# Attention through packed keys, then a squared-ReLU layer: another order for everything up to batch 1's first layer

## The chip, the cores and the metric

The kernel runs on one core of one Trainium2 chip. The metric is the device time of one execution in microseconds (us). A profile is one execution recorded by the hardware profiler. Its span is counted from the first to the last recorded instruction; the time of the execution is a little longer.

The core's engines are TensorE (PE in the profile; PEld is its weight loads), VectorE (DVE), ScalarE (ACT), GpSimd (POOL) and SyncE (SP). Each works through its own list of instructions in order and waits on semaphores of the others.

## What is computed

Eight batches of eight heads, 576 queries, keys and values of width 64, and 32 pack vectors `p` for each head. All inputs are float32.

```python
def sm_attn(qq, kk, vv):
    s = scale * np.matmul(qq, kk.transpose(0, 1, 3, 2))
    s = s - np.max(s, axis=-1, keepdims=True)
    a = np.exp(s)
    a = a / (np.sum(a, axis=-1, keepdims=True) + 1e-09)
    return np.matmul(a, vv)
p_packed = sm_attn(p, k, v)
out = sm_attn(q, p_packed, p_packed)
```

The result, brought to 4608 rows of 512, is `x`; the output is `relu(x @ w_in)**2 @ w_out` with `w_in` 512 x 2048 and `w_out` 2048 x 512.

## The kernel before, in words

The heads of a batch are handled as two quads of four. The first attention gives a packed matrix of 32 rows for each head; since it is key and value of the second one, `x @ w_in` is worked out as `a2 @ (packed @ w_in)`: the products "wp" of the packed matrix with W_in come first, and layer 1 multiplies the second softmax with them. The 576 tokens of batches 0 and 1 are cut into a first part of 256 and a second part of 320 (`CUTS`), and their softmax is done in these parts.

**The order is written out by hand.** `ORDER` (line 50) is a string of words, and `run` (line 768) turns each word into instructions in turn. Every engine executes its instructions in the order in which the words name them. A word may end in the engine for its vector work (`:v` VectorE, `:a` ScalarE, `:p` GpSimd); without an ending it is VectorE, or whatever the step has fixed. The first digit behind the letters is the batch, the next one the quad. The words that matter here:

- `Lk`, `Lv`: load keys, values (line 288). `LA`, `LB`: load both quads' queries of a batch, tokens of the first or second part (272). `Wi`n c: load a piece of W_in (253); n is the columns 0 to 255, 256 to 511 or 512 to 1023 of the half c. `Wo`: load a quarter of W_out (260). All of these are issued on the POOL queue, in front of and between GpSimd's own work. `pf`: load `p` of batches 0 and 1 on the SP queue. `Pr`, `Px`, `Pt`, `Pu`: the other batches' `p`.
- `I`: the identity for transpositions by TensorE, made on GpSimd. `P0`, `P1`: scale, cast and transpose `p` of batch 0 or 1 (VectorE, lines 231 and 235).
- `Z`n.m: n idle products of 512 columns and m of 256 on TensorE (line 331). Nothing reads them.
- First attention: `kT` transposes keys (VectorE, 351), `s1` scores (TensorE, 375), `m1` maximum (VectorE, 401), `x1` exponential (ScalarE, 413), `eT` transposes it on TensorE (433) and `eo` copies that out (421 on VectorE, 419 on ScalarE), `rd` reciprocal (444), `pv` product with the values (457), `pp` the scaled result (470), `bd` its transposition on VectorE (478), `pt` and `po` the one on TensorE and its copy (496).
- Second attention, A for the first part and B for the second: `qA`, `qB` transpose queries (VectorE, 363), `zA`, `zB` scores of both quads (TensorE, 375), `tA` transposes them (518), `mA` maximum (523), `sA` subtraction (529), `xA` exponential (ScalarE, 535), `uA` sum and reciprocal (541, 543), `aA` scaling (549), `TA` transposition (563), and the same with B.
- `wa`, `wb`, `w0`, `w1`: products with columns 0 to 255, 256 to 511, 0 to 511, 512 to 1023 of both halves of W_in (574); `Wa` and so on copy them out.
- Layer 1: `h`b.part.block is a product of two matmuls (590), `r` its relu (595 on ScalarE, 597 on VectorE), `q` the square of a pair of blocks (633 ScalarE, 635 VectorE or GpSimd). Layer 2: `o`tile.j two matmuls (648), `c` the copy out, `d` the store (679).

The POOL queue's loads use eight semaphores in turn, so that a load waits until the one eight places before it has landed. PSUM is shared out twice: before the first `h` three banks for attention and one for idle products, from the first `h` on two banks "x" and two "y" (`STAGES`). A product of batch 0's layer 1 takes a bank of x or y by the parity of its block and waits until the relu that last read that bank is through. Two larger buffers hold scores and wp products in turn.

Of the kernel before, what the change touches and what calls it, by code (L numbers as in the profile page):

```python
# [59 lines left out]
r0.1.15:v h0.1.4 r0.0.7:a Lv20 h0.1.6 m110 r0.1.4:a h0.1.5 r0.1.6:a h0.1.7 m111 h0.1.12 q0.0.3:a o2.0 x110 r0.1.5:v o2.1  # L60
r0.1.12:v q0.1.7:p o0.0 x111 o3.0 r0.1.7:a eT10 q0.1.6:a o0.1 Pr q0.1.2:v eT11 q0.1.3:v eo10:a o1.0 rd1 eo11:v o3.1 pv1
o1.1 pp1 o0.2 pt1 o1.2 bd1 po1:a o3.2 qA11 w011 w111 qA10 W011:a o0.3 W111:v o2.2 Lv21 o1.3 qB10 zA1 qB11 w010 o2.3 tA11
W010:a tA10 o3.3 mA11 zB1 mA10 sA11 w110 o0.4 sA10 tB11 W110:a o2.4 tB10 o1.4 mB11 xA11 o0.5 xA10 mB10 o1.5 uA10 o2.5
Lk20 sB11 o0.6 uA11 o0.7 xB11 aA10 o1.6 c0:a aA11 o1.7 sB10 o3.4 TA10 c1:a d0 TA11 o2.6 uB11 xB10 h1.0.1 Lk21 h1.0.6 Px
o2.7 r1.0.1:v d1 r1.0.6:v o3.5 aB11 h1.0.0 c2:a h1.0.2 Pt o3.6 r1.0.0:a TB11 o3.7 r1.0.2:a d2 Lk31 Pu:v q1.0.0:a h1.0.4
h1.0.3 c3:a o4.0 r1.0.3:v r1.0.4:a o5.0 kT20 q1.0.1:a h1.0.7 d3 h1.0.5 uB10 o5.1 r1.0.5:a o4.1 r1.0.7:v q1.0.2:a aB10
# [31 lines left out]
h4.0.10 q4.0.6 r4.1.2:a pv5 d17 r4.0.10:a h4.0.7 Lv61 q4.1.1 h4.0.15 r4.0.7:a o19.0 q4.0.5 r4.0.15:a pp5 o19.1 q4.0.3
o19.2 Lv71 bd5 h4.0.8 pt5 bs5:v h4.1.11 r4.0.8:a o18.3 po5:v q4.0.4 h4.1.1 s25 r4.1.11:a r4.1.1:v o18.4 qT60 h4.1.0
o18.5 t251 h4.1.6 o19.3 r4.1.0:a t250 r4.1.6:a o18.6 q4.1.0 h4.0.14 h4.1.10 m251 r4.0.14:a w050 r4.1.10:a w150 q4.0.7  # L100
W050:a h4.1.4 m250 h4.1.7 o18.7 r4.1.4:v W150:a o19.4 r4.1.7:v o19.5 q4.1.5 c18:a o19.6 q4.1.3 sb50:v o19.7 d18 h4.1.8
qT61 c19:a o20.0 x250 h4.1.5 sb51:v o21.0 d19 r4.1.5:a o20.1 r4.1.8:a su50 o21.1 x251 h4.1.12 q4.1.2 h4.1.9 r4.1.12:a
# [720 lines left out]
```

## Time and profile before

| | us |
|---|---|
| median of 3 runs | 243.33 (243.23 to 243.66) |
| time of the profiled execution | 243.35 |
| its span | 241.5 |
| TensorE busy | 235.4 |
| VectorE busy | 203.0 |
| ScalarE busy | 142.0 |
| GpSimd busy | 74.8 |

A row of the timeline gives start, duration, engine, line, operation, what is written and read, the number of instructions merged, and in brackets the idle time of the engine before it and what ended it. A row of the table by stages gives the stretch and its length, then busy time and number of instructions of PE, PEld, DVE, ACT and POOL, the granted clock, the share of the DMA engines and their GB/s. Line numbers are those of the kernel before; in the changed kernel each is two higher, since `ORDER` has two lines more.

### The profile page before, as it was taken

To read this page: it belongs to the slowest core of one execution; us is meant where nothing else is said; L and a number is where in the kernel's file an instruction comes from. 1 tells how busy PE (TensorE), PEld (TensorE's weight loads), DVE (VectorE), ACT (ScalarE), POOL (GpSimd) and SP (SyncE) were. 2 spreads that over 40 slices of the span, in tenths; PEclk is the share of its full clock that TensorE was granted. 3 is DMA by queue.
4 is the path that set the end of the run, shared out by engine and by line. 5 is a ranking of instruction groups with operands and counts; after the bars stand their busy time and mean duration, and the time that the engine had idled before them with its cause. 6 is when DMAs were issued, how large, how long until landed. Compare 5 with 4: busy or idle time off the path is not lost.

```text
span 241.5 us, 6098 instructions
## 1 busy us (share of the span) xinstructions
PE 235.4 (97%) x2415; PEld 125.9 (52%) x2415; DVE 203.0 (84%) x459; ACT 142.0 (59%) x308; POOL 74.8 (31%) x123
## 2 busy tenths in 40 slices
PE   8998899999999999999999999999999999999994
PEld 3544564456544564456555554465545644555542
DVE  2679986999998889989998889997899879987740
ACT  2216993697897557955693647774495346733300
POOL 8637783594585262044303340002000000000000
PEclk9999999999999999999999999999999999999999
DMA  6999999999999979259932974217113111111224
GB/s 103 189 199 210 202 206 206 181 209 210 194 169 212 236 103 136 51 71 209 107 86 28 206 107 66 62 34 105 37 24 76 46 46 43 43 46 43 50 61 109
DMA packets 33404, 28.51 MB, mean 118 GB/s; under 512 B 8160, under 2 KB 28384, under 8 KB 33376
## 3 DMA queue, kind: packets, MB, share of 16 engines
q0 software_dynamic: 26848, 18.55, 54.2%
q1 hardware_dynamic: 6384, 9.51, 14.8%
q8 instruction: 19, 0.31, 0.5%
q14 instruction: 9, 0.07, 0.1%
q10 hardware_dynamic: 144, 0.07, 0.1%
HBM read 37.22 MB, written 9.44 MB: 193 GB/s over the span
## 4 chain that ended last, share of the span: by engine, by line
PE 91%; DMA 4%; ACT 2%; DVE 1%; SPq 0%; issue 0%; POOL 0%; POOLq 0%
PE ps_o L648 50%; PE ps_h L590 26%; PE ps_wp L574 4%; PE ps_idle L335 3%; PE ps_s L375 3%; DMA k_b<-in_k_dram 2%; PE ps_e1T L433 2%; PE ps_pv L457 1%; DMA out_dram<-o_sb 1%; ACT r L595 1%; ACT wp L419 1%; SPq L679 0%; PE ps_ppT L496 0%; ACT gT L633 0%; DVE kT L351 0%
## 5 line engine op out<-in xcount | busy, mean ns | idle before, releaser
L648 PE MATMUL ps_o<-w_out_bf,gT 128*128 128x512 bf16 (+1 forms) x576 | 147.3, 378 | 0.0
L590 PE MATMUL ps_h<-a2T,wp 128*128 128x288 bf16 (+2 forms) x512 | 89.9, 286 | 1.3 <-DVE rs L543 0.6
L595 ACT ACTIVATE r<-ps_h 128x288 bf16<-128x288 f32 (+2 forms) x159 | 61.0, 415 | 47.2 <-PE ps_h L590 42.5
L648 PEld LDWEIGHTS <-gT 128*128 128x128 bf16 x576 | 54.4, 98 | 43.1 <-issue 3.4
L590 PEld LDWEIGHTS <-wp 128*128 128x128 bf16 x512 | 47.7, 98 | 42.4 <-issue 8.0
L597 DVE TENSOR_SCALAR r<-ps_h 128x288 bf16<-128x288 f32 (+2 forms) x97 | 41.9, 447 | 11.1 <-PE ps_h L590 10.5
L635 DVE TENSOR_TENSOR gT<-r 128x576 bf16<-128x576 bf16 (+2 forms) x104 | 45.1, 446 | 2.8 <-ACT r L595 1.8
L419 ACT CAST wp<-ps_wp 128x1024 bf16<-128x1024 f32 (+1 forms) x29 | 27.7, 974 | 9.0 <-PE ps_wp L574 8.9
L419 ACT COPY o_sb<-ps_o 128x512 f32<-128x512 f32 x26 | 15.2, 589 | 12.3 <-PE ps_o L648 10.1
L268 POOL DMA_DIRECT2D k_b<-in_k_dram x28 | 15.2, 544 | 16.5 <-DVE kT L351 7.3
L268 POOL DMA_DIRECT2D q_b<-in_q_dram x16 | 11.0, 690 | 28.8 <-DVE qT L363 25.4
L313 POOL DMA_DIRECT2D v_b<-in_v_dram x12 | 9.4, 779 | 31.5 <-PE ps_pv L457 30.5
L335 PE MATMUL ps_idle<-gT 128*128 128x512 bf16 (+1 forms) x59 | 16.1, 417 | 1.2 <-DVE gT L187 1.2
L413 ACT ACTIVATE e<-ps_s,nm 128x576 bf16<-128x576 f32 x16 | 11.8, 742 | 7.5 <-DVE nm L401 7.4
L633 ACT ACTIVATE gT<-r 128x512 bf16<-128x512 bf16 (+1 forms) x21 | 14.0, 690 | 0.5 <-DVE r L597 0.3
L535 ACT ACTIVATE e<-d 128x576 f32<-128x576 f32 (+2 forms) x20 | 11.7, 599 | 4.1 <-DVE d L529 3.9
L351 DVE STREAM_TRANSPOSE kT<-k_b 128x576 uint32<-128x576 uint32 x16 | 12.3, 767 | 0.6 <-DMA k_b<-in_k_dram 0.6
L363 DVE STREAM_TRANSPOSE qT<-q_b 128x576 uint32<-128x576 uint32 (+2 forms) x20 | 12.4, 633 | 0.0
L541 DVE TENSOR_REDUCE sums<-e 128x18 f32<-128x576 f32 (+2 forms) x20 | 12.2, 608 | 0.1
L401 DVE TENSOR_REDUCE nm<-ps_s 128x1 f32<-128x576 f32 x16 | 11.5, 739 | 0.8 <-PE ps_s L375 0.7
L523 DVE TENSOR_REDUCE mx<-s 128x18 f32<-128x576 f32 (+2 forms) x20 | 11.6, 609 | 0.0
L529 DVE TENSOR_TENSOR d<-s,mx 128x576 f32<-128x576 f32 (+2 forms) x19 | 11.6, 631 | 0.0
(60 smaller groups left out, 179.3 us busy)
## 6 DMA issues: line engine op xcount, KB each, us to landing
out_dram<-o_sb SPq DMA_DIRECT2D x65, 128.0 KB, 2.9
v_b<-in_v_dram POOLq DMA_DIRECT2D x12, 256.0 KB, 5.5
w_out_bf<-in_moe_w_out_dram POOLq DMA_DIRECT2D x4, 512.0 KB, 12.4
q_b<-in_q_dram POOLq DMA_DIRECT2D x6, 288.0 KB, 5.3
q_b<-in_q_dram POOLq DMA_DIRECT2D x12, 144.0 KB, 5.7
k_b<-in_k_dram POOLq DMA_DIRECT2D x12, 108.0 KB, 4.1
gT<-in_v_dram POOLq DMA_DIRECT2D x4, 288.0 KB, 9.7
w_in_bf<-in_moe_w_in_dram POOLq DMA_DIRECT2D x4, 256.0 KB, 9.8
```

The costliest lines, as they stand in the source:

```text
L268: engine.dma_start(x[n:], s[:P - n])
L335: self.nc.tensor.matmul(ps[:, :m], lhsT=self.nought[:, :P], rhs=self.nought[:, :m], start=True, stop=True)
L351: self.nc.vector.transpose(t["kT"][:].rearrange("p s e -> p (s e)").bitcast(U32), t["k"][:].rearrange("p t d -> p (t d)").bitcast(U32))
L363: self.nc.vector.transpose(out.bitcast(U32), x.bitcast(U32))
L419: engine.copy(out, x)
L541: nc.vector.reduce_sum(out=sums[:, x], in_=t["e2"][:, x], axis=AX.X)
L590: self.nc.tensor.matmul(ps, lhsT=t["wp"][:, fb // n, fb % n * P:(fb % n + 1) * P], rhs=t["a2T"][:, s0:s1], start=(qd == 0), stop=(qd == se ...
L595: engine.activation(r, ps, ACT.Relu)
L597: engine.tensor_scalar_max(r, ps, 0.0)
L633: engine.activation(out, r, ACT.Square)
L635: engine.tensor_tensor(out=out, in0=r, in1=r, op=ALU.mult)
L648: self.nc.tensor.matmul(self.o[tt][:, e], lhsT=self.gT[:, fb, a:a + P], rhs=self.w_out_bf[:, fb, e], start=(i == 0), stop=(i == self.NFB - 1))
```

## The change

Only `ORDER` changes. From `h1.0.1`, batch 1's first product of layer 1, on the words are the same in both (an engine that was left to the default is now written out). Before that point the same words stand in another order, except for the idle products, and 30 words have another engine. The beginning, up to batch 1's first scores `s11`:

```diff
-pf Lk00 Lk01 Lv00 Lv01 I P0 LA0 P1 Wi00 kT00 Wi10 LB0 Z18.0 s100 Wi01 kT01 Wi11 m100 Z2.0 s101 x100 m101 Wi21 x101 Z7.0
-eT00 eo00:v Z1.0 eT01 rd0 eo01:v Wi20 Z2.0 pv0 pp0 qA01 Lk10 Z2.0 pt0 bd0 qA00 po0:a Z2.1 zA0 Lk11 tA00 tA01 mA01 mA00
-sA01:v xA01 sA00:v uA01 xA00 qB00 Wo0 qB01 aA01:p uA00 Z18.1 zB0 wa00 Lv11 tB00 tB01 aA00:p Wa00:a mB00 Z2.1 wa01 mB01
-sB00:p Wa01:a TA01 Z1.1 wb01 TA00 Lv10 wb00 xB00 sB01:v h0.0.8 h0.0.9 Wb01:a Wb00:v h0.0.1 h0.0.0 xB01 uB00 r0.0.8:a
-r0.0.1:a h0.0.2 uB01 r0.0.9:a aB00:p r0.0.0:a h0.0.3 r0.0.2:v q0.0.4:a h0.0.11 Wo2 aB01:v h0.0.10 q0.0.0:a TB00 TB01
-r0.0.3:a r0.0.10:v r0.0.11:a h0.1.0 h0.1.1 q0.0.1:v q0.0.5:a h0.1.9 r0.1.0:v h0.1.8 r0.1.1:a r0.1.9:v LA1 w100 w101
-q0.1.0:v r0.1.8:a h0.1.10 W100:v W101:a h0.1.11 h0.1.3 q0.1.4:p h0.1.2 r0.1.10:a r0.1.3:v r0.1.11:a h0.0.4 kT10 r0.1.2:a
-LB1 h0.0.13 r0.0.4:a h0.0.5 q0.1.1:a h0.1.14 r0.0.13:v q0.1.5:p h0.0.14 r0.0.5:v h0.1.13 r0.1.14:a kT11 h0.0.15
-r0.0.14:a h0.0.6 q0.0.2:a h0.0.12 Wo1 r0.0.15:v s11 r0.1.13:a r0.0.12:v r0.0.6:a Wo3 h0.1.15 q0.0.7:v q0.0.6:a h0.0.7
...
+pf Lk00 kT00 Lk01 P0 Z14.0 s100 kT01 m100 x100 I s101 Z2.1 eT00 LA0 m101 x101 qA01 eo00:a Z0.1 eT01 Lv00 qA00 P1 eo01:v
+Lv01 rd0 LB0 Z0.1 pv0 pp0 bd0 Z1.0 pt0 zA0 tA01 qB01 Wi00 qB00 tA00 Wi01 mA01 Wi11 Wi10 mA00 Z6.1 zB0 tB00 Wi20 po0:a
+sA01:v xA01 sA00:v Wi21 xA00 tB01 mB00 uA00 wa01 Lk11 uA01 mB01 wa00 Wa01:a Lk10 sB00:p Wa00:a aA00:p xB00 Z5.1 wb00
+Wb00:a aA01:p TA00 sB01:v xB01 wb01 TA01 h0.0.8 uB00 uB01 Wo0 aB01:v Wb01:a aB00:p Lv10 h0.0.1 Lv11 TB00 h0.0.9 r0.0.8:a
+h0.0.2 h0.0.10 r0.0.1:a r0.0.9:a h0.0.3 h0.0.11 r0.0.2:a h0.0.0 TB01 r0.0.10:a r0.0.11:a q0.0.4:v r0.0.0:a r0.0.3:a
+h0.1.8 q0.0.5:v r0.1.8:v h0.1.0 h0.1.9 q0.0.0:a h0.1.1 r0.1.9:a h0.1.10 r0.1.0:a w100 q0.0.1:v r0.1.1:v Wo2 W100:v w101
+h0.1.11 r0.1.10:a W101:a r0.1.11:v h0.1.2 q0.1.0:v kT11 h0.1.3 r0.1.3:a q0.1.4:p h0.1.14 r0.1.2:a h0.0.5 h0.0.13
+r0.1.14:a LA1 LB1 h0.0.4 h0.0.14 r0.0.5:a kT10 r0.0.13:a h0.1.13 r0.0.4:a h0.1.15 r0.1.13:v h0.0.12 q0.1.1:a r0.0.14:a
+Wo1 r0.0.12:a s11 h0.0.6 h0.0.7 q0.1.5:v r0.1.15:a h0.1.4 m110 r0.0.6:a h0.0.15 m111 r0.0.7:a q0.1.7:p x110 r0.0.15:v
...
```

On the POOL queue the loads now stand in the order keys, queries' first part, values, queries' second part, the four small pieces of W_in, its two large ones, batch 1's keys; before it was keys, values, queries' first part, two small pieces of W_in, queries' second part, the other two, the large ones, batch 1's keys. On VectorE `kT00` goes ahead of `P0`, `P1` behind the queries' transpositions, `bd0` directly behind `pp0`, and the second part's transpositions `tB` between those steps of the first part. `eo00` and `Wb00` go to ScalarE. The idle products are 33 instead of 59: 14 instead of 18 ahead of `s100`, 19 instead of 41 behind it. Between `s11` and `h1.0.1` the old order has seven products `h` of batch 0, the new one eight.

More of the change, by code (lines that the diff above doesn't have):

```diff
@@ L61 @@
[L61 to L65, printed above, removed]
@@ L67 @@
+o2.7 r1.0.1:v d1 r1.0.6:v o3.5 aB11:v h1.0.0 c2:a h1.0.2 Pt o3.6 r1.0.0:a TB11 o3.7 r1.0.2:a d2 Lk31 Pu q1.0.0:a h1.0.4
+h1.0.3 c3:a o4.0 r1.0.3:v r1.0.4:a o5.0 kT20 q1.0.1:a h1.0.7 d3 h1.0.5 uB10 o5.1 r1.0.5:a o4.1 r1.0.7:v q1.0.2:a aB10:v
 h1.0.10 h1.0.8 q1.0.3:v r1.0.10:a o4.2 kT21 Lq2 h1.0.9 r1.0.8:a o5.2 r1.0.9:a h1.0.12 TB10 s12 q1.0.4:v r1.0.12:a
@@ L98 @@
[L98 to L102, printed above, removed]
@@ new lines @@
+q2.1.6:v q2.1.7:v h3.0.5 h3.0.2 qT41 r3.0.5:a o12.6 h3.0.0 r3.0.2:v Lq6 o11.6 r3.0.0:a o12.7 h3.0.1 h3.1.1 r3.0.1:v
+c12:a o11.7 r3.1.1:v s14 d12 c11:a q3.0.0:v h3.0.4 kT50 h3.0.3 r3.0.4:a o13.0 r3.0.3:a m140 d11 h3.0.9 Lk60 o14.0
+r3.0.9:a q3.0.1:v h3.1.3 x140 kT51 h3.1.0 o14.1 r3.1.3:a m141 o13.1 Lk70 r3.1.0:a h3.0.8 q3.0.2:v eT40 x141 h3.0.7
+r3.0.8:v o13.2 eo40:v r3.0.7:a h3.0.6 q3.1.0:v o14.2 q3.0.4:v r3.0.6:a eT41 rd4 q3.0.3:v h3.0.11 eo41:a h3.1.2 r3.0.11:v
+o14.3 r3.1.2:v o13.3 h3.0.12 h3.0.10 q3.1.1:v pv4 r3.0.10:a r3.0.12:v o14.4 Lv51 pp4 h3.0.13 q3.0.5:v h3.0.14 r3.0.13:a
@@ new lines @@
+aT40 aT41 o16.7 qT50 o15.6 c16:a h4.0.1 h4.0.4 Lq7 r4.0.1:v o15.7 d16 r4.0.4:v o17.0 c15:a h4.0.3 h4.0.2 r4.0.3:v o17.1
+r4.0.2:a d15 s15 q4.0.1:v h4.0.0 kT60 h4.0.9 o17.2 r4.0.0:a m151 o17.3 r4.0.9:a h4.0.6 m150 o17.4 r4.0.6:a h4.1.3
+q4.0.0:v x151 o17.5 kT61 o18.0 x150 o17.6 r4.1.3:v Lk71 h4.0.5 h4.0.13 rd5 r4.0.5:a o18.1 r4.0.13:v eT50 h4.0.11 eo50:v
+h4.0.12 eT51 q4.0.2:v o17.7 r4.0.12:v r4.0.11:a o18.2 eo51:a c17:v h4.1.2 h4.0.10 q4.0.6:v r4.1.2:a pv5 d17 r4.0.10:a
+h4.0.7 Lv61 q4.1.1:v h4.0.15 r4.0.7:a o19.0 q4.0.5:v r4.0.15:a pp5 o19.1 q4.0.3:v o19.2 Lv71 bd5 h4.0.8 pt5 bs5:v
@@ new lines @@
+h4.1.11 r4.0.8:a o18.3 po5:v q4.0.4:v h4.1.1 s25 r4.1.11:a r4.1.1:v o18.4 qT60 h4.1.0 o18.5 t251 h4.1.6 o19.3 r4.1.0:a
+t250 r4.1.6:a o18.6 q4.1.0:v h4.0.14 h4.1.10 m251 r4.0.14:a w050 r4.1.10:a w150 q4.0.7:v W050:a h4.1.4 m250 h4.1.7 o18.7
+r4.1.4:v W150:a o19.4 r4.1.7:v o19.5 q4.1.5:v c18:a o19.6 q4.1.3:v sb50:v o19.7 d18 h4.1.8 qT61 c19:a o20.0 x250 h4.1.5
+sb51:v o21.0 d19 r4.1.5:a o20.1 r4.1.8:a su50 o21.1 x251 h4.1.12 q4.1.2:v h4.1.9 r4.1.12:a w151 a250:v r4.1.9:a w051
+h4.1.15 W151:a su51 o20.2 o21.2 r4.1.15:a q4.1.4:v o21.3 W051:a a251:v o20.3 h4.1.14 aT50 h4.1.13 aT51 s16 r4.1.14:a
@@ new lines @@
+q6.0.4:v q6.1.0:v h6.0.12 h6.1.6 r6.0.12:v o28.2 o28.3 r6.1.6:v h6.0.13 o27.4 h6.1.7 r6.0.13:v s27 r6.1.7:a o27.5
+q6.0.6:v t270 h6.1.3 o27.6 r6.1.3:a t271 h6.1.11 o27.7 m270 h6.1.2 r6.1.11:a o28.4 c27:a q6.1.3:v o28.5 r6.1.2:a m271
+h6.1.12 d27 h6.1.4 r6.1.12:a o29.0 q6.1.1:v sb70:v r6.1.4:a o28.6 o29.1 sb71:v x270 o28.7 q6.1.2:v h6.1.8 c28:a su70
+w171 w071 x271 d28 h6.1.9 o30.0 r6.1.8:v W171:a su71 o30.1 o30.2 W071:a a270:v o30.3 h6.1.15 r6.1.9:a a271:v o29.2
+h6.1.10 r6.1.15:a q6.1.4:v o29.3 r6.1.10:a aT70 h6.1.13 h6.1.14 aT71 o30.4 r6.1.13:a q6.1.5:v r6.1.14:a o29.4 q6.1.6:v
@@ L132 @@
+r7.1.8:v o31.7 o32.5 r7.1.3:v c31:a h7.1.10 q7.1.1:v h7.1.6 d31 r7.1.10:v o33.0 r7.1.6:a o32.6 h7.1.12 h7.1.14 o33.1
+r7.1.12:v r7.1.14:a o32.7 h7.1.7 c32:v h7.1.9 r7.1.7:a o33.2 r7.1.9:a h7.1.11 d32 q7.1.3:v o34.0 q7.1.4:v h7.1.13
+r7.1.11:v o33.3 r7.1.13:a o34.1 q7.1.5:v q7.1.6:v h7.1.15 o33.4 r7.1.15:v o33.5 o33.6 q7.1.7:v o34.2 o34.3 o33.7 o34.4
+c33:v o34.5 o34.6 o34.7 d33 o35.0 c34:v o35.1 o35.2 d34 o35.3 o35.4 o35.5 o35.6 o35.7 c35 d35
 """
```

96 lines of the change are left out of this document (41 added, 55 removed).

## Prediction

> **What bounds the kernel now.** First the page: its head, then the busy share of the DMA engines in 40 slices of 6.04 us.
>
> ```profile
> span 241.5 us, 6098 instructions
> ...
> DMA  6999999999999979259932974217113111111224
> ```
>
> The loads keep the DMA engines full from the second slice to the thirteenth, some 78 us. An order of loads can therefore bring one piece earlier only by bringing another later. Next the busy time by stage, at the stage where the two orders meet again (from batch 1's scores `s11` to its first products of layer 1, `h1.0.1`):
>
> ```profile
> 30.00:48.80 18.80, 18.80 (x250) 9.18 (x248) 15.61 (x41) 12.20 (x26) 11.30 (x18) 1.00 1.37 197
> ```
>
> TensorE's column reads 18.80 of 18.80 us. From 30 us on TensorE is the bound, and what it does there is the same in both kernels. So the change can win or lose only ahead of that: by when TensorE reaches batch 1's scores (`s11`), and how much work it still has then. Hence the timeline of TensorE from the first product of layer 1 to `s11`:
>
> ```profile
> 21.28 1.03 PE L590 MATMUL ps_h<-a2T,wp 128*128 128x256 bf16 x8
> 22.90 1.20 PE L590 MATMUL ps_h<-a2T,wp 128*128 128x256 bf16 x8 [0.58 <-DVE rs L543]
> 24.45 1.56 PE L590 MATMUL ps_h<-a2T,wp 128*128 128x320 bf16 x8 [0.35 <-DVE a2T L563]
> 25.93 0.62 PE L574 MATMUL ps_wp<-w_in_bf,ppT 64*32 64x512 bf16 x16
> 26.49 1.26 PE L590 MATMUL ps_h<-a2T,wp 128*128 128x320 bf16 x8
> 28.04 2.54 PE L590 MATMUL ps_h<-a2T,wp 128*128 128x256 bf16 x18 [0.29 <-ACT r L595]
> 30.51 0.70 PE L375 MATMUL ps_s<-kT,pT 32*32 32x192 bf16 x48
> ```
>
> Three waits stand in brackets; ahead of 21.28 TensorE does little but idle products. What releases the first product and the 24.45 row is VectorE, so its timeline comes last:
>
> ```profile
> 7.76 0.78 DVE L351 STREAM_TRANSPOSE kT<-k_b 128x576 uint32<-128x576 uint32 x1 [0.60 <-DMA k_b<-in_k_dram]
> 8.46 1.62 DVE L401 TENSOR_REDUCE nm<-ps_s 128x1 f32<-128x576 f32 x2
> 11.27 0.55 DVE L421 COPY e1T<-ps_e1T 96x768 bf16<-96x768 bf16 x1 [1.19 <-PE ps_e1T L433]
> 11.75 0.15 DVE L444 RECIPROCAL rden<-den 128x2 f32<-128x2 f32 x1
> 11.82 0.55 DVE L421 COPY e1T<-ps_e1T 96x768 bf16<-96x768 bf16 x1
> 12.87 0.42 DVE L470 TENSOR_TENSOR pp<-ps_pv,rden 128x256 bf16<-128x256 f32 x1 [0.49 <-PE ps_pv L457]
> 13.21 0.43 DVE L363 STREAM_TRANSPOSE qT<-q_b 128x256 uint32<-128x256 uint32 x1
> 13.57 0.20 DVE L478 STREAM_TRANSPOSE ppd<-pp 128x64 uint32<-128x64 uint32 x1
> 13.69 0.40 DVE L363 STREAM_TRANSPOSE qT<-q_b 128x256 uint32<-128x256 uint32 x1
> 14.63 0.78 DVE L518 STREAM_TRANSPOSE s<-ps_s 128x256 f32<-128x256 f32 x2 [0.54 <-PE ps_s L375]
> 15.45 0.75 DVE L523 TENSOR_REDUCE mx<-s 128x8 f32<-128x256 f32 x2
> 16.11 0.75 DVE L529 TENSOR_TENSOR d<-s,mx 128x256 f32<-128x256 f32 x2
> 17.01 0.42 DVE L541 TENSOR_REDUCE sums<-e 128x8 f32<-128x256 f32 x1
> 17.46 0.20 DVE L543 RECIPROCAL rs<-sums 128x8 f32<-128x8 f32 x1
> 17.58 0.85 DVE L363 STREAM_TRANSPOSE qT<-q_b 128x320 uint32<-128x320 uint32 x2
> 18.36 0.38 DVE L541 TENSOR_REDUCE sums<-e 128x8 f32<-128x256 f32 x1
> 18.77 0.20 DVE L543 RECIPROCAL rs<-sums 128x8 f32<-128x8 f32 x1
> 19.14 0.91 DVE L518 STREAM_TRANSPOSE s<-ps_s 128x320 f32<-128x320 f32 x2 [0.17 <-PE ps_s L375]
> 19.98 0.84 DVE L523 TENSOR_REDUCE mx<-s 128x10 f32<-128x320 f32 x2
> 20.73 0.49 DVE L563 STREAM_TRANSPOSE a2T<-a 128x128 uint32<-128x128 uint32 x2
> ```
>
> Read it as one chain: the last load of keys (7.76), a stretch of short waits on TensorE, and from 14.63 to 21.22 VectorE with hardly a gap, after which the first product starts at 21.28.
>
> **The change part by part.** All times are in the profiled execution, 243.35 us with its span of 241.5, level with the median of 243.33.
>
> *Keys and first scores: 0.* `Lk00` and `Lk01` are still the first two loads, so the second transposition of keys still waits for its load until 7.76. `kT00` now stands ahead of `P0` on VectorE, which delays `s100`; but the maxima start behind `kT01` at 8.46 in either order.
>
> *`qA01`, `qA00` and `P1` into a gap: 0.* VectorE is idle for 1.19 us ahead of 11.27. The two transpositions of queries take 0.36 + 0.40 there. `P1` is a scaling of 128x128 and a transposition of 128x64, each between nothing and its nearest larger row (0.42 for 128x256, 0.20 for 128x64). All three together end by about 11.4, ahead of `eo01`, since `eo00` goes to ScalarE. Its price there is that of the same copy for batch 1, in the fence below (0.80 against 0.55); ScalarE has nothing else then. If the cover failed, `pv0` would be late by at most the 0.25 between the two.
>
> ```profile
> 22.47 1.20 ACT L595 ACTIVATE r<-ps_h 128x256 bf16<-128x256 f32 x4
> ...
> 35.72 0.80 ACT L419 COPY e1T<-ps_e1T 96x768 bf16<-96x768 bf16 x1
> ```
>
> *Loads: -0.1.* The POOL queue holds eight loads in flight, and its ninth and later ones show when an earlier one is in: the row that waits for the queries' first piece, and the row that waits for their second.
>
> ```profile
> 12.33 0.56 POOL L268 DMA_DIRECT2D k_b<-in_k_dram  x1 [0.73 <-DMA q_b<-in_q_dram]
> ...
> 17.30 0.78 POOL L261 DMA_DIRECT2D w_out_bf<-in_moe_w_out_dram  x1 [1.92 <-DMA q_b<-in_q_dram]
> ```
>
> The first piece (`LA0`) was fifth in line and was in at 12.3. Now it is third and `Lv01` is fifth with the same bytes ahead of it, so the values are in at about 12.2; `pv0`'s second half needs them and `eo01` (12.37), so they barely hide. `pp0` starts near 12.8 instead of 12.87. `LB0`, eighth before, is now sixth: at the page's rate, some 200 KB per us, its 320 KB need 1.6 us, so it is in at 13.8; if it takes the 2.4 that the row at 17.30 would leave it behind two pieces of W_in of 1.3 each, at 14.5. W_in's small pieces follow, two by 17, four by 19.5, where `wa` and `wb` use them; from there on the bytes in line are the old ones.
>
> *`bd0` straight behind `pp0`: -0.45 more.* Now `zA0` waits for the second query transposition to end (13.69 + 0.40 = 14.09), and VectorE reads its result 0.54 later. After the change `zA0` waits for `pp0` (12.8 + 0.34 = 13.14) and, on TensorE, for `pt0` (two products, some 0.4 with the hand-over, an estimate), while `bd0` (0.20) ends beside it: 13.54, and `tA01` starts at 14.08 instead of 14.63.
>
> *VectorE up to `TA01`: +0.1.* From start to start: `tA` 2 x 0.41, `qB` 2 x 0.39, `mA` 2 x 0.33, `sA` 2 x 0.38, sums and reciprocals 2 x 0.58, `tB` 2 x 0.42, `mB` 2 x 0.38, `TA` 2 x 0.25, and one subtraction of the second part (`sB01`) that now stands ahead of `TA01`, 0.45 (an estimate: 1.25 times `sA`'s). Sum 6.7, against 6.59 from 14.63 to 21.22. `TA01` ends near 20.8, and the first product of layer 1 starts there: **0.45 earlier**. `qB01` meets its load (14.5) just in time.
>
> *Second part of the tokens: -0.75 more.* When `TA01` ends, VectorE has done the second part's transpositions, maxima and subtraction; left are two sums (0.6 each), one `aB` (0.5) and two `TB` (0.28 each), so `TB01` ends at 23.0. ScalarE does eight relus in a row from 21.6 (behind the copies of `wb`), 0.30 each by the row at 22.47; the fifth frees the bank that `h0.1.8` needs, at 23.2. So the second part starts at 23.25 instead of 24.45: **1.2 earlier**.
>
> *To `s11` and beyond: +0.25.* Eight products of the second part, W_in's wide half and a third group follow as before, ScalarE and VectorE sharing relus and squares otherwise but in about the same sum (11 relus go to ScalarE and 7 leave it, four squares leave and three come). I carry the 1.2 to `s11`, at 29.3. Behind it the new order has eight products of batch 0 left and the old one seven: one costs 2.54/9 = 0.28. The rest of the way is TensorE's own, so the end comes **0.95 earlier**: 243.35 - 0.95 = 242.4.
>
> *Idle products: 0.* 59 become 33. Those behind `s100` fill waits; 19 of them stand between `zA0` and `zB0` today, and `zB0`'s own operand is ready only at 18.43 anyway.
>
> **TensorE's clock.** The idle products show two speeds:
>
> ```profile
> 5.01 0.15 PEld L335 LDWEIGHTS <-gT 128*128 128x128 bf16 x1 [0.28 <-issue]
> 5.44 1.44 PEld L335 LDWEIGHTS <-gT 128*128 128x128 bf16 x7 [0.28 <-issue]
> ```
>
> Until 5.44 one comes every 0.43 us, then every 0.21: half speed for the first 4.25 us of work (from 1.19). With 23 idle products fewer behind the first scores, TensorE idles for some 5 us more out of 14, in gaps of up to 1.2 us (an estimate from the times above). No row of this trace shows what such gaps do. The Trainium skill, "TensorE: Matmul & The Clock Gate", section "What's actually happening", says that the clock halves only after an idle window of about 3.4 us; by that rule the sum stays 242.4. The same page's section "A second HAM failure mode: psum-queue depth-cycling" speaks against the change: frequent short idling between groups can make the clock swing; by that the third rival below holds.
>
> **The rivals.**
> 1. *The queries' second piece is late.* The change doesn't bring `LB0` in by 14.5. Being sixth speaks for it; that a load behind others took 2.4 us instead of 1.6 speaks against. If it lands at 15.5, `qB01`, which stands second in the VectorE stretch, holds all behind it for 1 us: first product at 21.8, second part at 24.25, `s11` 0.2 earlier at best, and with the one product more the end is where it was: 243.3.
> 2. *Given back to ScalarE.* The relus and squares up to `s11` are on engines that are nearly full from 20 to 32 us. If ScalarE reaches the relus that free the banks 0.6 later than I have it (two relus' worth), the 0.95 falls to 0.35: 243.0.
> 3. *The clock falls* (slower). One mechanism: too little work between 9 and 20 us halves TensorE's clock until 4.25 us of work have passed. Then `zA0` on VectorE's chain takes 0.4 longer and `zB0` delays it by 0.1 (the rest has slack); the first eight products, at 0.43 each, take 3.4 instead of the 2.4 that eight relus take; in the 0.85 left of the 4.25 two products of 320 tokens lose 0.2 each. Together 1.9: 243.35 - 0.95 + 1.9 = 244.3. It outweighs the gain only if the clock is low at the first product of layer 1; low only before that, it costs at most 0.5.
>
> **How the numbers follow.** A measurement of this kernel can tell about 0.2%, 0.5 us. Forecast 0.55: 242.4, between 241.7 (the product left over costs nothing, and the relus don't delay the second part) and 242.85. Rival 1: 0.12. Rival 2: 0.15, half of it beyond 0.2%. Rival 3: 0.13. The remaining 0.05 is a load of W_in or W_out that TensorE now reaches 1 us too early, up to 243.8. Faster by over 0.2%: 0.55 and a part of rival 2, 0.61; within: 0.21; slower: 0.18. The range runs from 241.7 to 244.0: 244.3 and beyond are left out.
>
> **What would show it.** First product of layer 1 at 20.8 and first product of the 320 tokens at 23.25; `tA01` at 14.1 and no load among the releasers of the `qB` transpositions; `s11` at 29.3; TensorE full from there. Wrong are: weight loads of idle products or of the first products 0.43 apart behind 6 us (rival 3), a DMA ahead of `qT` (rival 1), ScalarE as releaser of `ps_h` for more than 0.6 in all between 23 and 30 us (rival 2).

## The result, and the profile after

| | before | after |
|---|---|---|
| median, us | 243.5 (243.23 to 243.71, 4 runs) | 241.76 (241.65 to 242.43, 4 runs) |
| ratio, 95% interval | | 0.9935 [0.9913, 0.9957] |
| profiled execution, its span | 243.35, 241.5 | 241.65, 239.8 |

The changed kernel is faster: by 1.7 us between the medians, by 0.65% (1.6 us) in the ratio. Its page has less busy time on TensorE (fewer idle products) and on VectorE, and more on ScalarE:

```profile
PE 227.4 (95%) x2355; PEld 123.4 (51%) x2389; DVE 200.8 (84%) x455; ACT 144.6 (60%) x313; POOL 73.4 (31%) x122
```

TensorE's timeline, the same places as before:

```profile
12.95 0.36 PE L459 MATMUL ps_pv<-gT,e1T 96*32 96x64 bf16 x24 [0.97 <-DMA gT<-in_v_dram]
...
14.14 0.42 PE L377 MATMUL ps_s<-qT,ppd 32*32 32x256 bf16 x16
...
20.47 0.27 PE L592 MATMUL ps_h<-a2T,wp 128*128 128x256 bf16 x1
21.27 3.96 PE L592 MATMUL ps_h<-a2T,wp 128*128 128x256 bf16 x25 [0.52 <-DVE a2T L565]
...
26.92 2.24 PE L592 MATMUL ps_h<-a2T,wp 128*128 128x320 bf16 x16 [0.22 <-ACT wp L421]
29.09 0.70 PE L377 MATMUL ps_s<-kT,pT 32*32 32x192 bf16 x48
...
47.34 0.60 PE L592 MATMUL ps_h<-a2T,wp 128*128 128x256 bf16 x4
```

The first products of layer 1 start where they did (21.27 against 21.28, one matmul ahead). But then 25 matmuls run in one row, both parts of the tokens in it, where the old order had eight, a wait of 0.58, eight and a wait of 0.35. `s11` comes at 29.09 instead of 30.51, 1.42 earlier, and `h1.0.1` at 47.34 instead of 48.80, 1.46 earlier. A new wait stands at 12.95: the second half of the values. VectorE shows why nothing is won ahead of 21.27 and much behind it:

```profile
13.38 0.42 DVE L472 TENSOR_TENSOR pp<-ps_pv,rden 128x256 bf16<-128x256 f32 x1 [1.23 <-PE ps_pv L459]
13.84 0.25 DVE L480 STREAM_TRANSPOSE ppd<-pp 128x64 uint32<-128x64 uint32 x1
14.63 0.45 DVE L520 STREAM_TRANSPOSE s<-ps_s 128x256 f32<-128x256 f32 x1 [0.55 <-PE ps_s L377]
15.01 0.86 DVE L365 STREAM_TRANSPOSE qT<-q_b 128x320 uint32<-128x320 uint32 x2
...
20.91 0.30 DVE L565 STREAM_TRANSPOSE a2T<-a 128x128 uint32<-128x128 uint32 x1
...
22.97 0.56 DVE L565 STREAM_TRANSPOSE a2T<-a 128x160 uint32<-128x160 uint32 x2
```

`pp0` comes 0.51 later than before (13.38 against 12.87), `tA01` at the same 14.63. From there to the end of `TB01` it is 8.90 us (to 22.97 + 0.56). In the old kernel it was 9.99, from 14.63 to 24.62 (24.06 + 0.56):

```profile
21.52 0.68 DVE L421 CAST wp<-ps_wp 128x512 bf16<-128x512 f32 x1
...
23.36 0.38 DVE L597 TENSOR_SCALAR r<-ps_h 128x256 bf16<-128x256 f32 x1
...
24.06 0.56 DVE L563 STREAM_TRANSPOSE a2T<-a 128x160 uint32<-128x160 uint32 x2
```

The difference, 1.09, is close to the time of two instructions that left VectorE for ScalarE, the copy `Wb00` (0.68) and the relu `r0.0.2` (0.38), 1.06 together. In the changed kernel ScalarE takes eight relus in a row, 0.29 each:

```profile
21.87 2.34 ACT L597 ACTIVATE r<-ps_h 128x256 bf16<-128x256 f32 x8
```

From `s11` to `h1.0.1` both kernels need the same time; the table by stages, the old kernel's row first:

```profile
30.51:48.80 18.29, 18.29 (x246) 8.96 (x245) 15.10 (x40) 11.69 (x25) 10.79 (x18) 1.00 1.37 197
```

```profile
29.09:47.34 18.25, 17.96 (x244) 9.22 (x247) 14.28 (x40) 13.75 (x28) 9.82 (x15) 1.00 1.34 196
```

So the gain is made between `tA01` and `s11` and passes through to the end.

### The profile page after: what moved, and what is told of

Same layout as the page of the kernel before. It is cut to its first block, busy times and chain, and to the rows that moved or that the text cites. A ratio compares the mean times of both kernels' runs of the same rounds, so it can differ in the third digit from the quotient of the medians.

```text
span 239.8 us, 6008 instructions
## 1 busy us (share of the span) xinstructions
PE 227.4 (95%) x2355; PEld 123.4 (51%) x2389; DVE 200.8 (84%) x455; ACT 144.6 (60%) x313; POOL 73.4 (31%) x122
## 4 chain that ended last, share of the span: by engine, by line
PE 85%; DVE 5%; DMA 4%; issue 2%; ACT 2%; POOL 1%; ACTq 0%; POOLq 0%
PE ps_o L650 50%; PE ps_h L592 26%; DMA gT<-in_v_dram 4%; PE ps_wp L576 3%; PE ps_s L377 3%; PE ps_e1T L435 2%; PE ps_pv L459 1%; DVE mx L525 1%; DVE d L531 1%; ACT r L597 1%; DVE s L520 1%; DVE qT L365 1%; PE ps_ppT L498 1%; DVE gT L637 0%; ACT wp L421 0%
## 5 line engine op out<-in xcount | busy, mean ns | idle before, releaser
L650 PE MATMUL ps_o<-w_out_bf,gT 128*128 128x512 bf16 (+1 forms) x544 | 141.3, 378 | 2.0 <-issue 0.5
L597 ACT ACTIVATE r<-ps_h 128x288 bf16<-128x288 f32 (+2 forms) x163 | 61.8, 413 | 48.0 <-PE ps_h L592 43.9
L599 DVE TENSOR_SCALAR r<-ps_h 128x288 bf16<-128x288 f32 (+2 forms) x93 | 40.6, 450 | 11.4 <-PE ps_h L592 10.5
L637 DVE TENSOR_TENSOR gT<-r 128x576 bf16<-128x576 bf16 (+2 forms) x106 | 45.7, 444 | 2.1 <-ACT r L597 1.2
L421 ACT CAST wp<-ps_wp 128x1024 bf16<-128x1024 f32 (+1 forms) x31 | 29.1, 961 | 7.2 <-PE ps_wp L576 7.2
L353 DVE STREAM_TRANSPOSE kT<-k_b 128x576 uint32<-128x576 uint32 x16 | 12.2, 769 | 4.9 <-DMA k_b<-in_k_dram 4.9
L635 ACT ACTIVATE gT<-r 128x640 bf16<-128x640 bf16 (+1 forms) x20 | 13.3, 694 | 0.5 <-DVE r L599 0.3
L576 PE MATMUL ps_wp<-w_in_bf,ppT 64*32 64x512 bf16 (+1 forms) x272 | 10.7, 369 | 1.4 <-DVE s L520 0.8
```

Source lines behind the costliest of these rows:

```text
L421: engine.copy(out, x)
L576: self.nc.tensor.matmul(ps[NP * g:NP * g + NP, c, :f1 - f0], lhsT=t["ppT"][D * c:D * c + D, NP * h:NP * h + NP], rhs=self.w_in_bf[D * c:D ...
L597: engine.activation(r, ps, ACT.Relu)
L599: engine.tensor_scalar_max(r, ps, 0.0)
L635: engine.activation(out, r, ACT.Square)
L637: engine.tensor_tensor(out=out, in0=r, in1=r, op=ALU.mult)
```

## Experiments

Each changes only words of `ORDER`. After the result two theories stood. **Theory E**: the gain comes from the engines, from what left VectorE between `tA01` and `TB01`. **Theory O**: it comes from the order on VectorE, which brings the second part's scores, maxima and the wp products forward. Rival 3, the clock, and the order of the loads were open beside them. One table for all, from the profiled executions: the start of `tA01`, the time from there to `s11`, the time from `s11` to the end of the span, and the median of all runs with the ratio to the kernel before, run beside it.

| kernel | `tA01` | to `s11` | to the end | median | ratio |
|---|---|---|---|---|---|
| before | 14.63 | 15.88 | 210.99 | 243.28 to 243.5 | |
| after | 14.63 | 14.46 | 210.71 | 241.76 | 0.9935 [0.9913, 0.9957] |
| two back on VectorE | 13.54 | 17.39 | 210.77 | 243.38 | 0.9996 [0.9980, 1.0013] |
| new order, old engines | 13.90 | 19.55 | 212.55 | 247.90 | 1.0183 [1.0154, 1.0212] |
| old order, new engines | 14.79 | 17.14 | 211.67 | 245.45 | 1.0097 [1.0074, 1.0120] |
| values first | 15.06 | 15.44 | 210.80 | 241.81 | 0.9943 [0.9918, 0.9968] |
| after, filled | 14.18 | 14.45 | 210.77 | 241.73 | 0.9934 [0.9920, 0.9949] |
| no late idle products | 14.86 | 15.57 | 210.77 | 242.56 | 0.9969 [0.9955, 0.9983] |
| values first, filled | 14.49 | 14.63 | 211.08 | 241.99 | 0.9949 [0.9934, 0.9964] |
| old order, loads only | 14.26 | 15.88 | 210.86 | 243.29 | 1.0001 [0.9991, 1.0011] |
| filled, two back | 14.33 | 15.99 | 210.78 | 242.80 | 0.9972 [0.9960, 0.9983] |
| filled, old VectorE order | 14.20 | 15.82 | 210.78 | 242.54 | 0.9966 [0.9955, 0.9977] |
| values first, `pp0` first | 14.77 | 14.84 | 210.99 | 241.82 | 0.9939 [0.9924, 0.9954] |

Read the columns apart. The last of the three times hardly moves, but for the two kernels where words behind `s11`, too, have an engine chosen for the other order. The first scatters by over a microsecond between kernels with the same words up to `tA01` (13.54 and 14.63), and with it single times. The second shows the mechanism.

**1. Two back on VectorE.**

```diff
-Wb00:a
+Wb00:v
-r0.0.2:a
+r0.0.2:v
```

> The changed kernel with two words back on VectorE: the copy of the second small wp product (Wb00, 0.68 us there) and the relu of h0.0.2 (0.38 us). Theory E (engines: the second part's softmax ends earlier since these two left VectorE): TB01 ends 1.06 us later, the first product of 320 tokens 1 us later, time 241.76 + 1.0 = 242.8. Rival O (order: tB, mB and sB stand earlier, which is what brings the second part forward): at most 0.2 us, 241.8 to 242.0.

Measured 243.38 (242.26 to 243.85): the whole gain is gone, more than these two should cost. The profiled execution (243.48) shows a second thing. On TensorE:

```profile
17.51 0.62 PE L576 MATMUL ps_wp<-w_in_bf,ppT 64*32 64x256 bf16 x15 [1.92 <-DMA w_in_bf<-in_moe_w_in_dram]
18.07 2.53 PE L337 MATMUL ps_idle<-gT 128*128 128x512 bf16 x6
```

and on VectorE:

```profile
21.01 0.69 DVE L423 CAST wp<-ps_wp 128x512 bf16<-128x512 f32 x1 [1.99 <-PE ps_wp L576]
```

A piece of W_in was late, TensorE idled for 1.92, and the six idle products behind it took 2.53, at half the clock; at the full clock these six (five of 512 columns, one of 256) take 1.36. `Wb00`, now on VectorE, waited 1.99 for its product behind them. The mean granted clock was 0.986 to 0.993 in eight of the twelve runs (medians 243.68 in these, 242.54 in the other four). So this run mixes the two instructions with the clock, and experiment 9 repeats it without that.

**2. New order, old engines.** All 30 words get their old engine back; three of them:

```diff
-Wb00:a r0.0.10:a q0.0.4:v
...
+Wb00:v r0.0.10:v q0.0.4:a
...
```

> The words in the new order, all 30 words that changed engine back on their old one. Theory E: the gain of 1.7 us falls to 0.7 or less, 242.8 or more, with VectorE as the releaser of the first product of 320 tokens. Rival O: most of the gain stays, 242.2 or less.

Measured 247.90 (246.89 to 249.26), 4.6 slower than before; 247.0 and 246.89 in the two runs at the full clock. TensorE's waits, summed over the run (who waited for whom: us in all, times, the longest), with the old kernel's line numbers:

```profile
PE ps_h L590 <- DVE r L597: 2.2, 3, 1.6
PE ps_h L590 <- DVE a2T L563: 1.4, 3, 0.9
...
PE ps_h L590 <- DVE wp L421: 1.1, 1, 1.1
```

Each of these names VectorE: it now has relus and copies among the second part's softmax, and TensorE waits for all three kinds of its work. Between them in the list stand 1.4 us for pieces of W_in. At the full clock the order alone costs 3.7. The result is on theory E's side (242.8 or more) and far from theory O's, but a loss as large as this was in neither.

**3. Old order, new engines.** The same 30 words in the old kernel, the other way round (`Wb00:a`, `r0.0.10:a` and so on in the old order).

> The words in the old order with the old idle products, the 30 words on their new engines. Theory E: 242.4 to 243.0 (1.06 us off VectorE, but ScalarE then does Wb00 ahead of xB01, 0.58 us, and 0.25 more for eo00 ahead of pv0). Rival O: no gain, 243.3 or more.

Measured 245.45 (245.39 to 246.90), 2.2 slower. Now it is ScalarE:

```profile
PE ps_h L592 <- ACT r L597: 1.9, 3, 1.1
```

In the old order the copies of the wp products come late on ScalarE, and the relus put behind them start at 23.12 and hold the banks. This is theory O's side (243.3 or more) and 2.5 us beyond theory E's. So experiments 2 and 3 speak for one theory each. Neither half of the change gains alone: order +4.6, engines +2.2, both together -1.7.

**4. Values first.** The first queries are loaded fifth, as in the old kernel, the values third and fourth.

```diff
-... s101 Z2.1 eT00 LA0 m101 x101 qA01 eo00:a Z0.1 eT01 Lv00 qA00 P1 eo01:v Lv01 rd0 LB0 Z0.1 pv0 pp0 bd0 Z1.0 ...
+... s101 Z2.1 eT00 m101 x101 eo00:a Z0.1 eT01 Lv00 P1 eo01:v Lv01 rd0 LA0 qA01 LB0 Z0.1 pv0 pp0 bd0 qA00 Z1.0 ...
```

> The changed kernel with batch 0's values loaded ahead of the queries' first part, as before the change, and the two transpositions of those queries later on VectorE (one behind rd0, one behind bd0). If the wait of 0.97 us for the values at pv0 is on the path: pp0 0.5 us earlier, tA01 at 14.2 to 14.4 instead of 14.63, time 241.3 to 241.5. If it is hidden (the queue only changes which of the two loads is late, or ScalarE's relus set the pace from 21.9 us on): 241.7 to 241.8, with tA01 near 14.6 or the relus where they were.

Measured 241.81 (241.14 to 243.05), no different from the changed kernel. Its seven runs fall apart by the clock: 242.48, 242.89 and 243.05 at a mean of 0.993, and 241.14 to 241.81 at 0.998 and above, medians 1.6 apart. The profiled one is the slowest, and its timeline shows what half a clock does there:

```profile
14.37 0.63 PE L377 MATMUL ps_s<-qT,ppd 32*32 32x256 bf16 x16 [0.31 <-DVE qT L365]
...
17.60 0.48 PE L377 MATMUL ps_s<-qT,ppd 32*32 32x320 bf16 x16
```

`zA0` takes 0.63 instead of 0.42. `zB0` stands behind seven idle products (six of 512 columns, one of 256) and starts 3.23 us after `zA0`, in the changed kernel 1.86 (14.14 to 16.00): at half speed the filling itself is in the way. The clock is not all that is late in this execution: VectorE waits 1.13 us for the queries' first part, until 12.95, and `tA01` is at 15.06.

**5. After, filled.** Eleven more idle products, 44 in all: four ahead of `s100`, one ahead of `pt0`, three ahead of each `wa`.

```diff
-Z14.0 s100 ... Z1.0 pt0 ... uA00 wa01 Lk11 uA01 mB01 wa00
+Z18.0 s100 ... Z2.0 pt0 ... uA00 Z3.0 wa01 Lk11 uA01 mB01 Z3.0 wa00
```

> The changed kernel with 11 more idle products in its gaps: four behind the first fourteen, three ahead of each of wa01 and wa00, one ahead of pt0. Theory C (in some executions TensorE's granted clock falls for one stretch of about 3.4 us, since too few idle products are left; mean clock 0.993 instead of 1.000): mean clock 0.998 or more in every run, times between 241.3 and 242.0, median 241.6. Rival L (the spread of the changed kernel comes from loads that land at other times): the same spread as before the fill, up to 242.5, with mean clocks of 0.993 among the runs.

Measured 241.73 (241.17 to 242.10), level with the changed kernel; the mean clock is 1.000 in each of the six runs (the changed kernel: 1.000, 0.997, 0.993 and 0.993 with 241.65, 241.66, 241.86 and 242.43). The profiled one, 241.17, is the changed kernel's timeline 0.46 earlier, from the values on:

```profile
12.50 0.36 PE L459 MATMUL ps_pv<-gT,e1T 96*32 96x64 bf16 x24 [1.09 <-DMA gT<-in_v_dram]
...
20.81 3.96 PE L592 MATMUL ps_h<-a2T,wp 128*128 128x256 bf16 x25 [0.53 <-DVE a2T L565]
...
28.63 0.70 PE L377 MATMUL ps_s<-kT,pT 32*32 32x192 bf16 x48
```

The values landed 0.45 earlier, and every row behind them and the end (0.48) came that much earlier. Filling holds the clock, but does not move the median here, and at the full clock the six runs still spread over 0.93.

**6. No late idle products.** Only the first 14 are kept; the other 19 go.

```diff
-s101 Z2.1 eT00 ... Z0.1 eT01 ... Z0.1 pv0 ... Z1.0 pt0 ... Z6.1 zB0 ... Z5.1 wb00
+s101 eT00 ... eT01 ... pv0 ... pt0 ... zB0 ... wb00
```

> The changed kernel with only the first fourteen idle products; the other nineteen are left out. Theory C: the clock falls in every execution, mean 0.985 to 0.993, 1 to 2 us slower than 241.7: 242.7 to 243.7. Rival N (idle products only fill waits and do nothing): 241.7 and a mean clock of 1.000.

Measured 242.56 (241.71 to 243.07), 0.8 above the filled kernel. The mean clock is 0.970 to 0.979 in all eleven runs; at 0.979 they take 241.71 to 242.28, at 0.970 to 0.972 they take 242.56 to 243.07. In the profiled one (242.98) the table by stages has the granted clock third from the end:

```profile
8.16:11.57 3.41, 1.82 (x44) 1.29 (x47) 2.92 (x8) 2.34 (x5) 1.10 (x2) 1.00 1.29 201
11.57:25.22 13.65, 8.51 (x132) 4.43 (x133) 10.50 (x32) 6.60 (x17) 7.74 (x12) 0.50 1.30 204
25.22:28.63 3.41, 3.19 (x33) 1.53 (x32) 3.05 (x7) 3.36 (x9) 2.05 (x3) 1.00 1.20 203
```

```profile
16.15 0.73 PE L377 MATMUL ps_s<-qT,ppd 32*32 32x320 bf16 x16 [1.36 <-DVE qT L365]
...
21.49 5.08 PE L592 MATMUL ps_h<-a2T,wp 128*128 128x256 bf16 x25 [0.42 <-DVE a2T L565]
```

The clock falls at 11.57 and is back at 25.22. The block of 25 matmuls, nearly all of it at half the clock, takes 5.08 instead of 3.96. This is rival 3 as it was described, low clock at the first product, at a price of 0.8 in the medians: 1.3 in the six runs at 0.970 to 0.972, 0.3 in the five at 0.979. The clock fell for longer than forecast and cost less.

**7. Values first, filled.** Experiments 4 and 5 together.

```diff
-eT00 LA0 ... Lv01 rd0 LB0 ... uA00 wa01
+eT00 ... Lv01 rd0 LA0 qA01 LB0 ... uA00 Z3.0 wa01
```

> The order with the values ahead of the queries' first part (as in the run of that order), and the same 11 more idle products. Theory C: the runs of that order at full clock (241.14 to 241.32) become all of them, 241.2 to 241.5, and it beats the changed kernel by 0.3 to 0.5. Rival L: still spread from 241.1 to 243, median 241.8.

Measured 241.99 (241.59 to 242.52) at a clock of 0.999 or more: the expected gain is missing. The values are there in time, and now the queries are not:

```profile
12.59 0.45 DVE L365 STREAM_TRANSPOSE qT<-q_b 128x256 uint32<-128x256 uint32 x1 [1.15 <-DMA q_b<-in_q_dram]
```

12.59 against the 12.50 of the values in experiment 5: in these two executions the fifth load in line is waited for, whichever it is. Why the four runs of experiment 4 at the full clock (241.14 to 241.81) were mostly faster than these six is open.

**8. Old order, loads only.** The kernel before with `LB0` ahead of W_in's pieces.

```diff
-LA0 P1 Wi00 kT00 Wi10 LB0 Z18.0
+LA0 P1 LB0 Wi00 kT00 Wi10 Z18.0
```

> The kernel before with one edit: the queries' second part loaded ahead of all pieces of W_in. By the reading that the new load order is worth nothing without the order on VectorE (there qB00 starts only behind uA01, at 17.58, and its load was in at 17.3): 243.2 to 243.6. By the reading that the load itself is the gain: 242.5 or less.

Measured 243.29 (242.75 to 243.69), ratio 1.0001 [0.9991, 1.0011]. The earlier load alone is worth nothing. It was in by 14.24, when the load that takes over its semaphore starts, against 17.30 before; but in the old order nothing asks for it before 17 us.

**9. Filled, two back.** Experiment 1 on the filled kernel.

```diff
-Wb00:a ... r0.0.2:a
+Wb00:v ... r0.0.2:v
```

> The changed kernel with the 11 more idle products, and Wb00 and the relu of h0.0.2 back on VectorE: the earlier trial of these two words without the clock falling. Theory E (VectorE's own work up to TB01 is what the second part waits for): mean clock 1.000 in every run, TB01 and the first product of 320 tokens 1.0 us later than in the filled kernel, 242.6 to 242.9. If most of the 1.6 us in the earlier trial was the clock: 242.0 or less.

Measured 242.80 (242.47 to 243.22) at a clock of 0.997 to 1.000: 1.1 above the filled kernel, or 0.9 by the two ratios (0.9972 against 0.9934), whose intervals are apart. VectorE, then TensorE:

```profile
20.40 0.69 DVE L423 CAST wp<-ps_wp 128x512 bf16<-128x512 f32 x1 [0.58 <-PE ps_wp L576]
```

```profile
21.36 0.27 PE L592 MATMUL ps_h<-a2T,wp 128*128 128x256 bf16 x1 [0.93 <-DVE a2T L565]
21.96 1.96 PE L592 MATMUL ps_h<-a2T,wp 128*128 128x256 bf16 x13 [0.33 <-DVE a2T L565]
24.36 0.65 PE L592 MATMUL ps_h<-a2T,wp 128*128 128x256 bf16 x4 [0.44 <-DVE r L599]
```

The copy waits for its product in VectorE's line (0.58) with both transpositions `TA` behind it, and the relu holds a bank (0.44). With that wait `TB01` ends 10.22 us behind `tA01` instead of 8.90, 1.32 more where 1.06 was expected. Theory E is shown, for about 1 us by the medians; the stretch from `tA01` to `s11` is 15.99, as long as in the kernel before (15.88).

**10. Filled, old VectorE order.** The engines stay; `qB`, `zB0`, `tB` and `mB` go back to their old places, and with `zB0` the old 19 idle products ahead of it, so that there are nine more in all (53). GpSimd, too, scales the first part ahead of subtracting the second again.

```diff
-tA01 qB01 Wi00 qB00 tA00 Wi01 mA01 Wi11 Wi10 mA00 Z6.1 zB0 tB00 Wi20 po0:a sA01:v xA01 sA00:v Wi21 xA00 tB01 mB00 uA00 Z3.0 wa01 ...
+tA01 Wi00 tA00 Wi01 mA01 Wi11 Wi10 mA00 Wi20 po0:a sA01:v xA01 sA00:v Wi21 xA00 uA01 qB01 qB00 uA00 Z18.1 zB0 tB00 tB01 mB00 wa01 ...
```

> The filled kernel with the second attention of batch 0 in the old order on VectorE (second part's queries transposed behind the first sum, zB0 behind 18 idle products, tB and mB behind the first part's sums; GpSimd scales the first part ahead of subtracting the second), engines as changed. Theory E: the same work ends at the same time, within 0.3 of the filled kernel, 241.5 to 242.0. Theory O (the earlier tB and mB are worth something by themselves): 242.4 or more, and a wait of TensorE for a2T or for relus between the first and second part.

Measured 242.54 (242.23 to 243.46): 0.8 above the filled kernel, ratio 0.9966 against 0.9934, the intervals apart again. Theory E alone is refuted, theory O holds beside it. On ScalarE and TensorE (line numbers one lower than in the changed kernel):

```profile
18.93 0.58 ACT L420 CAST wp<-ps_wp 128x512 bf16<-128x512 f32 x1 [2.21 <-PE ps_wp L575]
...
22.79 2.35 ACT L596 ACTIVATE r<-ps_h 128x256 bf16<-128x256 f32 x8
```

```profile
22.96 3.20 PE L591 MATMUL ps_h<-a2T,wp 128*128 128x256 bf16 x19 [0.56 <-ACT wp L420]
```

With `zB0` at 18.15 instead of 15.54 the wp products behind it on TensorE, their copies and then the relus are late: the relus start at 22.79, in experiment 5 at 21.41. These 1.38 match the 1.37 by which the stretch to `s11` is longer. The 19 idle products end only at 18.22, while the queries' transpositions end at 17.84, so of the 2.61 that `zB0` is late some 0.3 belong to the idle products and not to VectorE's order. The stretch, 15.82, is again that of the kernel before.

**11. Values first, `pp0` first.** Experiment 7 with `qA01` and `qA00` behind `bd0`, so that a late query load holds nothing but `zA0`.

```diff
-rd0 LA0 qA01 LB0 Z0.1 pv0 pp0 bd0 qA00
+rd0 LA0 LB0 Z0.1 pv0 pp0 bd0 qA01 qA00
```

> Values ahead of the queries' first part, filled, and pp0 and bd0 on VectorE ahead of both query transpositions, so that pp0 no longer stands behind a transposition that waits for its load. If that in-order wait took the gain of the values: pp0 near 11.9, tA01 at 14.0 instead of 14.5, 241.2 to 241.5, better than the changed kernel. If the fifth load in line is the bound whichever it is: tA01 at 14.3 or later, 241.7 or more.

Measured 241.82 (241.42 to 242.52), as the changed kernel. No load is waited for any more, but `zA0` waits for the transpositions:

```profile
14.28 0.42 PE L377 MATMUL ps_s<-qT,ppd 32*32 32x256 bf16 x16 [0.64 <-DVE qT L365]
```

`pp0` started 0.51 earlier than in the changed kernel (12.87), and two transpositions behind it (0.73) take it back. This execution (242.46) is one of the two slowest of six and began late: the 18 idle products ahead of the first scores lasted until 8.18, in experiment 5 until 6.70, and the maxima started at 8.86 instead of 8.41. So the trace shows the new wait, not what the order is worth; that is left to the medians. By them no kernel tried is clearly faster than the changed one.

## Why the prediction was right or wrong

The direction and the place were right, the size not: 0.95 was forecast, 1.7 measured. The median, 241.76, lies just inside the lower end of the range, 241.7, and that is in part luck: one step gave more than forecast, another charged what was not due, and the loads took back less than these two gave. Step by step:

- *Keys and first scores, 0*: right. The second transposition of keys starts at 7.70 (7.76), the maxima at 8.41 (8.46).
- *`qA` and `P1` into a gap, 0*: right. `eo01` starts at 11.52, before at 11.82.
- *Loads, -0.1*: **wrong in this execution.** The values' second half was forecast at 12.2 and is in at 12.95; `pp0` starts at 13.38, not 12.8. In other kernels with the same first loads it was in at 12.22 (experiment 2), 12.50 (5), 12.65 (9) and 12.80 (6), and in experiment 1, which shows no wait for it, by 11.85: the forecast lies inside a spread of 1.1, which the prediction did not allow for. `LB0` was in time; the `qB` row at 15.01 shows no wait, and rival 1 did not occur.
- *`bd0` behind `pp0`, -0.45*: right, but eaten by the loads. From `pp0` to `tA01` it takes 1.25 us (13.38 to 14.63), forecast 1.28, before 1.76.
- *VectorE up to `TA01`, +0.1*: 6.58 from 14.63 to 21.21, forecast 6.7, before 6.59.
- *Second part, -0.75 more*: the mechanism right, the size too small. From `tA01` to the end of `TB01` 8.90, forecast 8.92 (14.08 to 23.0). The relus take 0.29, forecast 0.30. But the first product of 320 tokens starts at 23.40, forecast 23.25, although `tA01` was 0.55 late: 8.77 behind `tA01`, not 9.17. ScalarE starts its eight relus 7.24 behind `tA01` (21.87), where the forecast had 7.52. So this step gave 1.05 (24.45 to 23.40), and that it nearly met the forecast time is luck.
- *To `s11` and beyond, +0.25*: **this step failed.** I charged the product left over behind `s11` and did not credit it ahead of `s11`. The old order has 25 products there and 7 behind, the new one 24 and 8: the sum to `h1.0.1` is 32 in both, so nothing is to be charged. From `s11` to `h1.0.1` it is 18.25 against 18.29; why the eighth product does not even lengthen that stretch is not shown. Without this step the forecast would have been 1.2 and 242.15.
- *Idle products, 0*: right at the median, 241.76 with 33 and 241.73 with 44; with only 14 the kernel is 0.8 slower. Behind the first scores there are 22 fewer (41 and 19), not 23, and the DMA engines are full up to the fourteenth slice, not the thirteenth; neither slip enters the sum.

In the profiled execution, then, the first part gave 0 instead of 0.45, the way from `tA01` to `s11` 1.42 instead of the 0.66 that the forecast had there (15.88 less 15.22), and the left-over product nothing. Of the 1.42, 1.00 are TensorE's waits (0.58 + 0.35 + 0.29 before, 0.22 now); the rest, 0.42, is about one product fewer ahead of `s11` (0.28 by the forecast's price) and the matmul that now starts at 20.47 (half a product). That is argued: the new order has two products of 256 tokens fewer there and one of 320 more, which by columns is less than 0.28. Behind `s11` the span is another 0.28 shorter; undisturbed kernels differ there by as much (210.71 to 211.08), so this stays unexplained.

Of the rivals, the second did not occur either: ScalarE holds TensorE for 0.22 between 23 and 30 us. The third occurs in part. Two of four runs of the changed kernel had a mean clock of 0.993 (241.86 and 242.43 against 241.65 and 241.66), too few to tell a price from the spread at the full clock, and without the late idle products the fall is there every time. Its price was put at 1.9 with a low clock at the first product and at 0.5 at most with a low clock only before it. In experiment 6 it was 1.3 in the runs with the longest fall and 0.3 in the others, and between the runs of experiment 4 it was 1.6, so the gain outlived it.

Shown by runs of their own: that the gain needs the two instructions off VectorE (0.9 to 1.1 by the medians and ratios of the filled kernel) and the interleaved order (0.8), and that the earlier load by itself gives nothing. These are two conditions of one gain, not shares that add up: without either, the stretch from `tA01` to `s11` is that of the kernel before (15.99 and 15.82 against 15.88). The traces put their price at 1.54 and 1.37, more than the medians do; the filled kernel's profiled execution, 241.17, is the fastest of its six, and where its median execution differs was not traced. Not tested by themselves: the other 28 words that changed engine, and `bd0` ahead of the queries' transpositions, whose 0.5 is read from the trace. Only argued: that the spread at the full clock (241.17 to 242.10 in the filled kernel) is the landing of the fifth load; two executions, the filled and the changed one, agree with it (0.45 at the values, 0.48 at the end).

## What to carry to other kernels

Where several engines work through one written order, the order and the choice of engine are one decision: each half alone made this kernel slower, by 4.6 us (3.7 at the full clock) and 2.2 us, and both together faster by 1.7. To forecast such a change, follow the one engine whose work in line releases the bound engine, and count the bound engine's work on both sides of every mark; a product that only moved across a mark cost nothing at the end here. Of loads that are waited for early, ask which is how far back in line: here swapping them only changed the name in the bracket.

## What the runs showed of the hardware

- **The clock falls without a long idle stretch.** In experiment 6 the granted clock is 1.00 up to 11.57 us, then 0.50 until 25.22. Since the first idle products TensorE's gaps ahead of that fall were at most 0.82; its longest, the 1.36 at 16.15, came when the clock was already low. But in the 3.41 us that ended with the fall TensorE was busy for only 1.82. The Trainium skill, "TensorE: Matmul & The Clock Gate", section "What's actually happening", has the clock halve after an idle window of about 3.4 us; if that means a window without matmuls, none is in this trace, and the clock of 0.50 from 11.57 us on contradicts it as a necessary condition. Its section "A second HAM failure mode: psum-queue depth-cycling", by which frequent short idling can make the clock swing, agrees. The length of 3.4 us itself does come back, in the next point.
- **It stays low for 3.41 us or a multiple.** It was low for 3.41 us each in the profiled executions of experiments 1 (17.42 to 20.84), 2 (31.86 to 35.28) and 4 (13.92 to 17.33), and for four times that, 13.65, in experiment 6. The mean clocks of single runs fit: 0.993 over some 241 us is one such stretch at half the clock, 0.979 is three, 0.971 four. In the 3.41 us ahead of each of the four falls TensorE was busy for 1.58, 1.44, 1.84 and 1.82. In experiment 2 it was also busy for 1.82 from 18.21 to 21.62 and kept its clock, so these traces give no sharp limit.
- **Filling works both ways.** With 44 idle products the mean clock was 0.997 or more in all 25 runs of experiments 5, 7, 9 and 11, with 33 in 10 of 23 (the changed kernel, experiments 1 and 4), with 14 in none of eleven. But once the clock is low, idle products that stand ahead of real work delay it: six took 2.53 us instead of 1.36 in experiment 1. The slow start does the same: there the first 14 took 6.14 us, in experiment 6 the same 14 took 4.93.
- **Loads land with a spread.** The fifth load of one and the same beginning was in by 11.85 us in one execution and at 12.95 in another, a spread wider than the gain that was forecast.
